# Attention and two expert layers on one core: the bias table by distance, stored with a shift per row

## The chip, the cores and the metric

One of the eight cores of a Trainium2 chip runs the whole program. The metric is the device time of one execution in microseconds (us). The kernel before was run three times: 969.26, 970.4 and 975.79 us, median 970.4. One more execution was profiled.

## The reference, cut to what matters

Three layers follow each other: attention with a learned bias, a layer of eight experts of which each token uses one, and a gated layer. The change is in the first, and there in the bias:

```python
B, H, S, D = 4, 8, 576, 64              # batch, heads, positions, head size; 32 hidden units
scores = scale * q @ k.T
psi_rel = log1p(abs(pos[:, None] - pos[None, :]))
psi_i = log1p(maximum(pos[:, None], 1.0))
x = (psi_rel / psi_i)[..., None]        # 576 x 576 x 1
h = maximum(x @ w1 + b1, 0.0)           # 576 x 576 x 32
bias = h @ w2                           # 576 x 576 x 8, the same for every batch
scores = scores + bias                  # then softmax over the last axis, and times v
```

For one query row i the bias is a function of the distance |i - j| alone; the row enters only through the factor 1 / psi_i. All data is float32.

## The kernel before, in words

**The bias stage** makes the bias of all eight heads once and puts it into three scratch tensors in device memory (`scr[0]`, `scr[1]`, `scr[4]`), from which attention loads it pair by pair of heads. There are 36 blocks of 16 query rows (`BLKS`): for c = 0 to 3 and k = 0 to 7 the rows c + 64k, c + 64k + 4, ... (every fourth row, so that c fits the order in which attention takes its rows), and for c = 4 and k = 0 to 3 sixteen adjacent rows from 512 + 16k.

For each block, `z_gen` makes four tiles z of 128 partitions (4 rows x 32 hidden units) by 576 columns: relu of a row's factor times a table of log distances, plus b1. The table stands in `ctab_sb` once per stride of rows, `toep4` and `toep1`, in a form in which a shifted window of 576 columns gives the distances of the rows at hand; the row's factor is a per-partition column of `sall`. Of the four tiles VectorE makes three (L853) and ScalarE one (L851); `ZACT` holds how many ScalarE makes, by block. On VectorE the bias is left out of the relu and made good by `off8`, a column chosen by the same number.

Three blocks later (`LA = 3`), `z_mm` multiplies the four tiles with the block-diagonal weights `w2bd` (128 x 32), each into its own 32 output partitions: 512 columns in one bank of PSUM (L866), 64 in the next (L868). That gives 16 rows x 8 heads = 128 partitions by 576. ScalarE evicts it (L875; for the last two blocks L878, with the end on VectorE, L881) into an output tile `ob`, and SyncE stores it (L872) as 128 rows of 2304 bytes. Tiles z rotate through the pools `pt0`, `E` and, in the first part of the stage (`cnt < 24`), `bias`; output tiles through `ph`, which has four buffers and is also where attention's `E` tiles come from.

`z_iter` runs `z_gen`, `z_mm` and, where `LBS` lists the iteration, one of the first pair's bias loads. 38 iterations (`Z0`) run ahead of attention, and the last one after unit 0's first scores. Between the iterations the list `extra` issues one piece each: the loads of v for the first pair (`load_v`, iterations 0 to 3), the constants of the gates (`consts`, iteration 6: two loads of the gates' weights in short pieces, one table and a memset on GpSimd), and unit 1's k and q (`load_u(0, 1)`, iterations 11 and 12). SyncE's queue issues all of these, in program order.

**Attention** takes 16 units (4 pairs of heads x 4 batches) of 5 steps. A step does the scores (L274, `s_pe`), the bias add with the row maximum on VectorE (L278, `s_max`, reading tiles of `load_bias`), the exponential on ScalarE (L283), and the transposes and the product with v of two steps earlier. Splitting q and k into a high and a low part for the next unit is GpSimd's work (L228 to L237, `prep_qk`); unit 0 runs on whole float32. Loads for later units and pairs stand in `dmaq` with due times, nine per unit, and two at most are issued in a step. `WARM` adds a few idle matmuls on the table in unit 0 (L951). After attention come the expert layer and the gated layer, whose matmuls (L598, L611, L1300, L1309, L1562) take most of the time. The order of all instructions is written out by hand.

## Time and profile before

| what | value |
|---|---|
| runs | 969.26, 970.4, 975.79 us; median 970.4 |
| profiled execution | 969.1 us, of it 967.3 us span from the first to the last instruction |
| mean granted TensorE clock | 0.999 |
| busy, share of the span | TensorE 98%, weight loads 84%, VectorE 71%, ScalarE 56%, GpSimd 12% |
| bias stage | 4.7 to 57.7 us |
| first bias add and first exponential of attention | 59.56 and 60.38 us |

Shares of the whole span mix stages with different limits; the stage of the change is 53 us of 967. In the rows below PE is TensorE's matmuls, PEld its weight loads, DVE VectorE, ACT ScalarE, POOL GpSimd, and SPq SyncE's queue, which issues the DMAs. L853 is line 853 of the kernel. A row of the timeline has the start, the time to the end of the last of its instructions, and in brackets how long the engine had been idle and on what; adjacent instructions overlap a little, so the pace is read from the starts.

### The profile page before, as it was taken

To read this page: it belongs to the slowest core of one execution; us is meant where nothing else is said; L and a number is where in the kernel's file an instruction comes from. 1 tells how busy PE (TensorE), PEld (TensorE's weight loads), DVE (VectorE), ACT (ScalarE), POOL (GpSimd) and SP (SyncE) were. 2 spreads that over 40 slices of the span, in tenths; PEclk is the share of its full clock that TensorE was granted. 3 is DMA by queue.
4 is the path that set the end of the run, shared out by engine and by line. 5 is a ranking of instruction groups with operands and counts; after the bars stand their busy time and mean duration, and the time that the engine had idled before them with its cause. 6 is when DMAs were issued, how large, how long until landed. Compare 5 with 4: busy or idle time off the path is not lost. (4 is left out here: it accounts for less than half of the span.)

```text
span 967.3 us, 19675 instructions
## 1 busy us (share of the span) xinstructions
PE 947.8 (98%) x7621; PEld 814.6 (84%) x7621; DVE 687.6 (71%) x1536; ACT 537.0 (56%) x1139; POOL 113.6 (12%) x112
## 2 busy tenths in 40 slices
PE   7999999999999999999999999999999999999997
PEld 3457777777668999999999899999999999999996
DVE  8977878878786577777556578777546677456663
ACT  8978778777775353534435443555434455345542
POOL 0954343434300000000000000000000000000000
PEclk9999999999999999999999999999999999999999
DMA  8873433343044476858654585420312510312212
GB/s 238 253 256 115 139 118 103 94 130 102 2 139 151 140 258 206 285 204 280 231 171 162 198 254 171 115 82 1 107 46 66 135 41 1 131 33 66 66 34 65
DMA packets 90815, 130.26 MB, mean 135 GB/s; under 512 B 13760, under 2 KB 48576, under 8 KB 90720
## 3 DMA queue, kind: packets, MB, share of 16 engines
q1 hardware_dynamic: 90240, 128.33, 41.4%
q8 instruction: 60, 0.98, 0.4%
q10 hardware_dynamic: 480, 0.66, 0.2%
q14 instruction: 35, 0.29, 0.1%
HBM read 93.50 MB, written 35.46 MB: 133 GB/s over the span
## 5 line engine op out<-in xcount | busy, mean ns | idle before, releaser
L278 DVE CUSTOM_DVE_ANT_0 E<-S,bias 128x576 f32<-128x576 f32 x128 | 91.8, 754 | 29.7 <-PE S L274 21.4
L283 ACT ACTIVATE E<-E,st 128x576 f32<-128x576 f32 x144 | 110.3, 769 | 1.1 <-DVE st L278 0.8
L1300 PE MATMUL Y<-fv,ws 128*128 128x384 f32 x540 | 108.8, 336 | 0.1
L1300 PEld LDWEIGHTS Y<-fv,ws 128*128 128x128 f32 x540 | 95.7, 188 | 3.2 <-issue 0.4
L385 PE MATMUL pv<-pt,rawv 128*64 128x320 f32 (+1 forms) x576 | 88.1, 422 | 0.0
L1562 PE MATMUL o<-ws,u 128*128 128x512 f32 x306 | 84.1, 394 | 0.0
L274 PEld LDWEIGHTS S<-kh,qz 64*128 64x128 f32 x540 | 52.4, 185 | 34.6 <-DVE st L278 18.9
L274 PE MATMUL S<-kh,qz 64*128 64x288 f32 x540 | 76.3, 322 | 1.6 <-DVE st L278 1.4
L600 ACT ACTIVATE qz<-T 128x288 fp32r<-128x288 f32 x63 | 25.8, 410 | 87.3 <-PE T L598 87.2
L1040 DVE TENSOR_TENSOR ws<-r,ws 128x512 fp32r<-128x512 f32 (+1 forms) x66 | 51.3, 778 | 32.0 <-ACT ws L1037 31.2
L1300 PE MATMUL X<-fr,ws 128*128 128x384 f32 x360 | 73.3, 338 | 0.0
L324 ACT ACTIVATE pt<-T 128x512 f32<-128x512 f32 (+3 forms) x112 | 50.7, 467 | 39.9 <-PE T L301 39.5
L1300 PEld LDWEIGHTS X<-fr,ws 128*128 128x128 f32 x360 | 65.0, 188 | 5.6
L1562 PEld LDWEIGHTS o<-ws,u 128*128 128x128 f32 x306 | 56.2, 188 | 6.6 <-DVE u L1355 0.4
L326 DVE COPY pt<-T 128x512 f32<-128x512 f32 (+3 forms) x112 | 55.8, 522 | 3.3 <-PE T L301 3.2
L598 PE MATMUL T<-xh,whl 128*128 128x288 f32 x256 | 56.9, 298 | 0.0
L611 PE MATMUL y<-qz,w2hl 128*128 128x288 f32 x384 | 56.5, 296 | 0.0
L611 PE MATMUL y<-qz,whl 128*128 128x288 f32 x384 | 56.4, 296 | 0.0
L601 DVE SCALAR_TENSOR_TENSOR qz<-T,qz 128x288 fp32r<-128x288 f32 x63 | 28.6, 454 | 38.4 <-ACT qz L600 37.9
L598 PE MATMUL T<-xh,w1hl 128*128 128x288 f32 x248 | 55.7, 300 | 0.0
L301 PE MATMUL T<-ident,E 64*128 64x64 f32 x1248 | 54.1, 222 | 0.0
L301 PEld LDWEIGHTS T<-ident,E 64*128 64x128 f32 x1248 | 51.2, 138 | 2.5 <-issue 0.8
(322 smaller groups left out, 2115.4 us busy)
## 6 DMA issues: line engine op xcount, KB each, us to landing
r<-wn SPq DMA_DIRECT2D x22, 512.0 KB, 4.8
bscr<-ob SPq DMA_DIRECT2D x36, 288.0 KB, 3.3
raww<-in_moe_w_dram SPq DMA_DIRECT2D x16, 512.0 KB, 6.0
bias<-bscr SPq DMA_DIRECT2D x14, 576.0 KB, 4.3
raww<-in_moe_w_dram SPq DMA_DIRECT2D x24, 256.0 KB, 4.5
raww<-in_moe_w_dram SPq DMA_DIRECT2D x8, 768.0 KB, 8.5
ro<-wn SPq DMA_DIRECT2D x22, 256.0 KB, 2.7
rawq<-in_qt_dram SPq DMA_DIRECT2D x16, 320.0 KB, 3.1
```

Source lines behind the costliest of these rows:

```text
L274: nc.tensor.matmul(t[:, f, 0:288], x[k, a], y[k, o], start=i == 0, stop=i == len(prods) - 1)
L278: nc.vector.tensor_tensor_reduce(out=E.rearrange("p (a b) -> p a b", a=2), in0=ps[:, :, 0:288], in1=bt[p, hh, c].rearrange("p (a b) -> p a ...
L283: nc.scalar.activation(E, E, AF.Exp, bias=st[:, 2 * c + hh:2 * c + hh + 1], scale=-1.0, accum_out=st[:, 10 + 2 * c + hh:11 + 2 * c + hh])
L301: nc.tensor.transpose(t[r][:, at:at + 64], E[k, o:o + 128], ident[k, k])
L324: nc.scalar.activation(o, x, AF.Copy)
L326: nc.vector.tensor_copy(o, x)
L385: nc.tensor.matmul(st["ps"][64 * hh:64 * hh + 64, 0:w], vt[p][:, hh, b, c, :], y, start=c == order[0], stop=c == order[4])
L598: nc.tensor.matmul(ps, wa[:, x, k], xs[k][y][:, o], start=k == 0 and i == 0, stop=k == 3 and i == 2)
L611: nc.tensor.matmul(hbuf["y"][d // 2][:, d % 2, 0:288], wb[:, x, d], t[:, y:y + 288], start=f == 0 and i == 0, stop=(one or f == 7) and i == 2)
L1040: return lambda: eng.tensor_tensor(l, t, h.bitcast(F32), ALU.subtract)
L1300: nc.tensor.matmul(bank, a[:, c], x[:, k], start=first and k == 0 and n == 0, stop=k == 1 and n == 2, skip_group_check=True)
L1562: nc.tensor.matmul(t, u, w, start=first and i == 0, stop=last and i == 2)
```

## The change

The table is now one row of log1p of the distances 0 to 577, after the 144 row factors, in one load. Each tile z has w columns, one for each distance that any of the block's 16 rows can have: L to the left and R to the right (`z_span`), w the larger of L + 1 and R, made even. The matmuls put the columns in order of position, L + R of them: those to the left read z backwards, those to the right forwards, with a cut at 512 for the bank of PSUM, so two or three pieces of four matmuls each. All 16 rows of a block have the same columns, and the store puts each row at its own shift: rows of the scratch tensors are 704 wide (`WB`), a row of a block 639 or 640 columns (591 for c = 4), and the row's step in memory is 704 plus the stride of the rows. Loads of the bias take columns 64 to 639 of each row; the tail's load becomes two, one per head of the pair.

Beside that, `ZACT` gives ScalarE no tile in every seventh block (VectorE makes all four there); the pool `bias` serves tiles z in blocks below 16 instead of 24; `LBS` has the first pair's four early bias loads at iterations 22, 24, 31 and 32 instead of 25, 27, 29 and 30; unit 1's k and q are issued at iteration 33; and the constants of the gates become an entry of `dmaq` with due time 27 (the first step of unit 3).

```diff
@@ -46,15 +46,14 @@
 QR, QX, QY, LP = 46, 52, 55, 6
 QL, QC = ((58, 55, 61), 58)
 F0, F1 = ((1, 2, 3, 5, 7), (0, 1, 2))
-ZACT = (1,)
-LBS = ((25, 1), (27, 0), (29, 2), (30, 3), (37, 5), (37, 6), (38, 4))
+ZACT = (1, 1, 1, 1, 1, 1, 0)
+LBS = ((22, 1), (24, 0), (31, 2), (32, 3), (37, 5), (37, 6), (38, 4))
 WARM = {1: 512, 2: 128, 3: 128}
 Z0 = 38
 
 
 BLKS = [(c, k) for c in range(5) for k in range(4 if c == 4 else 8)]
-C4, C1 = 499, 572
-W4, W1 = C4 + S, 60 + S
+TD, WB = S + 2, 704
 
 
 def both(f, g):
@@ -67,10 +66,17 @@
     return (512 + 16 * k + 4 * gq, 1) if c == 4 else (c + 4 * (16 * k + 4 * gq), 4)
 
 
+def z_span(bi):
+
+    c, k = BLKS[bi]
+    if c == 4:
+        return 527 + 16 * k, 64 - 16 * k
+    return 64 * k + (64 if k == 7 else 63), 576 - 64 * k
+
+
 def make_consts():
     r = np.repeat(np.arange(4), HID)[:, None]
-    t4 = np.log1p(np.abs(4 * r + C4 - np.arange(W4)[None, :]).astype(np.float32))
-    t1 = np.log1p(np.abs(r + C1 - np.arange(W1)[None, :]).astype(np.float32))
+    td = np.broadcast_to(np.log1p(np.arange(TD).astype(np.float32)), (128, TD))
     st = np.array([z_rows(bi, gq) for bi in range(len(BLKS)) for gq in range(4)])
     i = st[None, :, 0] + st[None, :, 1] * r
     linv = np.float32(1.0) / np.log1p(np.maximum(i, 1).astype(np.float32))
@@ -85,7 +91,7 @@
     cst2 = np.ones((128, 384), np.float32)
     cst2[:, 0:128] = np.triu(cst2[:, 0:128], 1)
     cst2[:, 128:256] = np.arange(128)
-    return {"ctab": np.concatenate([t4, linv, t1], 1).astype(np.float32), "cst": cst, "cst2": cst2}
+    return {"ctab": np.concatenate([linv, td], 1).astype(np.float32), "cst": cst, "cst2": cst2}
 
 
 def lay(inputs):
@@ -130,15 +136,13 @@
 
         ident = const.tile([128, 128], F32, name="ident")
         make_identity(nc, ident)
-        ctab_sb = ap.tile([128, NG + W4 + W1], F32, tag="pt1", bufs=2, name="ctab_sb")
-        toep4, toep1 = ctab_sb[:, 0:W4], ctab_sb[:, NG + W4:]
+        ctab_sb = ap.tile([128, NG + TD], F32, tag="pt1", bufs=2, name="ctab_sb")
+        dist = ctab_sb[:, NG:]
         w_s = const.tile([32, 10], F32, name="w_s")
         reps = ap.tile([32, 256], F32, tag="ph", bufs=EB, name="reps")
         rep_sb, w2rep = reps[:, 0:128], reps[:, 128:256]
         nc.sync.dma_start(w_s, ws)
-        for o in (slice(C4 - 48, NG + W4), slice(0, C4 - 48)):
-            nc.sync.dma_start(ctab_sb[:, o], ctab[:, o])
-        nc.sync.dma_start(toep1, ctab[:, NG + W4:])
+        nc.sync.dma_start(ctab_sb, ctab)
         cst_sb = const.tile([128, 84], F32, name="cst_sb")
         wg = const.tile([128, 4, 32], F32, name="wg")
         small = ap.tile([128, S], F32, tag="rb", bufs=1, name="small")
@@ -161,7 +165,7 @@
         for i, n in enumerate((128, 96, 64)):
             nc.scalar.activation(off8[0:n, i:i + 1], wps[0:n, 1, 0:1], AF.Copy, scale=8.0)
 
-        nc.vector.tensor_scalar(sall, ctab_sb[:, W4:W4 + NG], wcol[:, 0:1], None, ALU.mult)
+        nc.vector.tensor_scalar(sall, ctab_sb[:, 0:NG], wcol[:, 0:1], None, ALU.mult)
 
         xT = {}
         bt = {}
@@ -174,7 +178,8 @@
             def tail():
                 t = ap.tile([128, S], F32, tag="bias5", bufs=1, name="biast")
                 bt[p, 0, 4] = bt[p, 1, 4] = t
-                dq.dma_start(t, scr[4][2 * p:2 * p + 2].rearrange("h r j -> (h r) j"))
+                for h in range(2):
+                    dq.dma_start(t[64 * h:64 * h + 64], scr[4][2 * p + h, 0:64 * WB].rearrange("(r j) -> r j", j=WB)[:, 64:64 + S])
 
             def part(hh, g):
                 def f():
@@ -185,7 +190,7 @@
                         if i == 4:
                             bt[0] = pers.tile([128, NTOK], F32, tag="xT3", name="bias").rearrange("p (i a j) -> p i a j", i=2, a=2)
                         t = bt[0][:, i - 4]
-                    dq.dma_start(t, scr[g][:, 2 * p + hh].rearrange("c a j -> a c j"))
+                    dq.dma_start(t, scr[g][:, 2 * p + hh, 0:128 * WB].rearrange("c (a j) -> a c j", j=WB)[:, :, 64:64 + S])
                     for r in range(2):
                         bt[p, hh, 2 * g + r] = t[:, r]
                 return f
@@ -196,7 +201,7 @@
                         t = ap.tile([128, 2, S], F32, tag="bias", bufs=4, name="bias")
                         for i in range(2):
                             bt[p, hh, 2 + i] = t[:, i]
-                    dq.dma_start(bt[p, hh, 2 + r], scr[1][r, 2 * p + hh])
+                    dq.dma_start(bt[p, hh, 2 + r], scr[1][r, 2 * p + hh, 0:128 * WB].rearrange("(a j) -> a j", j=WB)[:, 64:64 + S])
                 return f
             rows = [part(0, 1), part(1, 1)] if p else [row(hh, r) for r in range(2) for hh in range(2)]
             return [part(0, 0), part(1, 0)] + rows[0:2] + [tail] + rows[2:]
@@ -817,7 +822,7 @@
         ld0 = load_v(0, nc.sync)
         for f in load_u(0, 0):
             f()
-        extra = ld0 + [lambda: None] * 6 + load_u(0, 1)
+        extra = ld0
 
         def consts():
             nc.sync.dma_start(cst_sb, cst)
@@ -825,28 +830,28 @@
             nc.gpsimd.memset(wg[:, :, 16:32], 0.0)
             nc.sync.dma_start(wg[:, :, 8:16], moe_w_output_gate.rearrange("(p d) e -> d p e", p=4))
 
-        extra.insert(len(extra) - 6, consts)
-
-        scr = {g: dram.tile([2, H, 128, S], F32, name=f"bscr{g}") for g in range(2)}
-        scr[4] = dram.tile([H, 64, S], F32, name="bscr4")
+
+        scr = {g: dram.tile([2, H, 129 * WB], F32, name=f"bscr{g}") for g in range(2)}
+        scr[4] = dram.tile([H, 65 * WB], F32, name="bscr4")
         zss = {}
 
         def z_gen(cnt):
             act = ZACT[cnt % len(ZACT)]
-            if cnt < 24 and cnt % 4 == 3:
+            if cnt < 16 and cnt % 4 == 3:
                 zt = [ap.tile([128, 2, S], F32, tag="bias", bufs=4, name="zk") for _ in range(2)]
                 zs = [zt[i // 2][:, i % 2] for i in range(4)]
-            elif cnt % 4 == 1 if cnt < 24 else cnt % 3 == 0:
+            elif cnt % 4 == 1 if cnt < 16 else cnt % 3 == 0:
                 zs = [ap.tile([128, S], F32, tag="E", bufs=4, name="ze") for _ in range(4)]
             else:
                 zt = ap.tile([128, 4, S], F32, tag="pt0", bufs=2, name="zp")
                 zs = [zt[:, i] for i in range(4)]
             zss[cnt] = zs
+            L, R = z_span(cnt)
+            w = max(L + 1, R)
+            w += w % 2
             for gq in (0, 3, 2, 1):
-                i0, sd = z_rows(cnt, gq)
                 g = 4 * cnt + gq
-                src = toep4[:, C4 - i0:C4 - i0 + S] if sd == 4 else toep1[:, C1 - i0:C1 - i0 + S]
-                z = zs[gq]
+                src, z = dist[:, 0:w], zs[gq][:, 0:w]
                 if gq >= 4 - act:
                     nc.scalar.activation(z, src, AF.Relu, bias=wcol[:, 1:2], scale=sall[:, g:g + 1])
                 else:
@@ -862,23 +867,28 @@
             else:
                 pt = pS.tile([128, 1024], F32, tag="S", name="bps")
                 ps = [pt[:, 0:512], pt[:, 512:1024]]
-            for gq in range(4):
-                nc.tensor.matmul(ps[0][32 * gq:32 * gq + 32, 0:512], w2bd, zs[gq][:, 0:512], start=True, stop=True)
-            for gq in range(4):
-                nc.tensor.matmul(ps[1][32 * gq:32 * gq + 32, 0:64], w2bd, zs[gq][:, 512:576], start=True, stop=True)
-            ob = ap.tile([128, S], F32, tag="ph", bufs=EB, name="ob")
+            L, R = z_span(cnt)
+            w = L + R
+            cuts = sorted({0, min(L, w), 512, w})
+            for u, v in zip(cuts, cuts[1:]):
+                for gq in range(4):
+                    z = zs[gq]
+                    x = z[:, L - v + 1:L - u + 1][:, ::-1] if v <= L else z[:, u - L:v - L]
+                    nc.tensor.matmul(ps[u // 512][32 * gq:32 * gq + 32, u % 512:u % 512 + v - u], w2bd, x, start=True, stop=True)
+            ob = ap.tile([128, WB], F32, tag="ph", bufs=EB, name="ob")[:, 0:w]
             def put():
-                dst = scr[4] if c == 4 else scr[c // 2][c % 2]
-                nc.sync.dma_start(dst[:, 16 * k:16 * k + 16, :].rearrange("h r j -> r h j"), ob)
+                dst, i0, sd = (scr[4], 512 + 16 * k, 1) if c == 4 else (scr[c // 2][c % 2], c + 64 * k, 4)
+                o = 16 * k * WB + 64 + i0 - L
+                nc.sync.dma_start(dst[:, o:o + 16 * (WB + sd)].rearrange("h (r j) -> r h j", r=16)[:, :, 0:w], ob)
 
             if not own:
-                nc.scalar.activation(ob, pt[:, 0:S], AF.Identity, bias=off8[:, act:act + 1], scale=8.0)
+                nc.scalar.activation(ob, pt[:, 0:w], AF.Identity, bias=off8[:, act:act + 1], scale=8.0)
                 put()
                 return
             nc.scalar.activation(ob[:, 0:512], ps[0], AF.Identity, bias=off8[:, act:act + 1], scale=8.0)
 
             def rest():
-                nc.vector.tensor_scalar(ob[:, 512:S], ps[1][:, 0:64], 8.0, off8[:, act:act + 1], ALU.mult, ALU.add)
+                nc.vector.tensor_scalar(ob[:, 512:w], ps[1][:, 0:w - 512], 8.0, off8[:, act:act + 1], ALU.mult, ALU.add)
                 put()
             if cnt == nb - 1:
                 late.append(rest)
@@ -903,13 +913,14 @@
 
         for cnt in range(Z0):
             z_iter()
-            n = -(-len(extra) // (Z0 - cnt))
-            for f in extra[:n]:
-                f()
-            extra = extra[n:]
+            if extra:
+                extra.pop(0)()
+            if cnt == 33:
+                for f in load_u(0, 1):
+                    f()
         dq = nc.sync
         mq = moe_early()
-        dmaq = []
+        dmaq = [(27, consts)]
         pe, ve = {}, {}
 
         def at_step(d, n, f):
...
```

## Rows read from the trace of the kernel before

**Rows 1.** Busy time of each engine by stretch, TensorE clock, DMA share and rate

```profile
core 0: us, PE busy (x) PEld busy (x) DVE busy (x) ACT busy (x) POOL busy (x), PEclk, DMA share, GB/s
4.70:57.70 53.00, 49.10 (x562) 22.74 (x564) 52.98 (x109) 50.32 (x71) 32.59 (x1) 1.00 0.87 266
30.00:42.00 12.00, 11.35 (x132) 5.45 (x131) 12.00 (x26) 11.26 (x18) 12.00 (x1) 1.00 0.71 196
44.00:55.00 11.00, 9.77 (x125) 5.56 (x123) 11.00 (x24) 10.83 (x16) 11.00 (x1) 1.00 1.01 357
80.00:100.00 20.00, 20.00 (x271) 14.40 (x268) 15.41 (x42) 15.13 (x38) 7.60 (x10) 1.00 0.45 141
```

**Rows 2.** Timeline, VectorE: the first tiles, the last ones, and what follows

```profile
4.72 1.56 DVE L853 TENSOR_SCALAR zp<-ctab_sb,sall,small 128x576 f32<-128x576 f32 x3
...
54.72 3.04 DVE L853 TENSOR_SCALAR zp<-ctab_sb,sall,small 128x576 f32<-128x576 f32 x6
57.66 0.29 DVE L881 TENSOR_SCALAR ob<-T,small 128x64 f32<-128x64 f32 x1
```

**Rows 3.** Timeline, ScalarE, one block of the bias stage

```profile
35.29 0.87 ACT L851 ACTIVATE zp<-ctab_sb,small,sall 128x576 f32<-128x576 f32 x1
36.05 0.73 ACT L875 ACTIVATE ob<-bps,small 128x576 f32<-128x576 f32 x1
36.67 0.87 ACT L851 ACTIVATE zk<-ctab_sb,small,sall 128x576 f32<-128x576 f32 x1
```

**Rows 4.** Timeline, from the bias stage to attention's first step

```profile
57.44 1.24 PE L274 MATMUL S<-rawk,rawq 64*128 64x288 f32 x8
...
59.56 0.76 DVE L278 CUSTOM_DVE_ANT_0 E<-S,bias 128x576 f32<-128x576 f32 x1 [1.61 <-DMA bscr<-ob]
...
59.79 0.69 ACT L878 ACTIVATE ob<-bps,small 128x512 f32<-128x512 f32 x1 [1.60 <-PE bps L866]
...
60.38 0.77 ACT L283 ACTIVATE E<-E,st 128x576 f32<-128x576 f32 x1
```

**Rows 5.** VectorE by line and shape: busy us and mean ns, then idle time before

```profile
L853 DVE TENSOR_SCALAR zp<-ctab_sb,sall,small 128x576 f32<-128x576 f32 x60 | 30.8, 578 | 0.0
...
L666 DVE TENSOR_SCALAR sel<-meta 128x128 f32<-128x128 f32 x5 | 1.4, 345 | 0.0
```

**Rows 6.** ScalarE by line and shape, columns as in rows 5

```profile
L324 ACT ACTIVATE pt<-T 128x512 f32<-128x512 f32 x64 | 38.3, 599 | 31.9 <-PE T L301 31.6
...
L875 ACT ACTIVATE ob<-bps,small 128x576 f32<-128x576 f32 x34 | 24.8, 731 | 1.5 <-PE bps L868 0.9 <-DMA bscr<-ob 0.5
...
L324 ACT ACTIVATE pt<-T 128x256 f32<-128x256 f32 x16 | 6.1, 382 | 7.9 <-PE T L301 7.9
```

**Rows 7.** Timeline, TensorE, one block of the bias stage

```profile
16.62 1.07 PE L866 MATMUL bps<-zk,small 128*32 128x512 f32 x8 [0.21 <-ACT ob L875]
...
17.50 0.30 PE L868 MATMUL bps<-zk,small 128*32 128x64 f32 x8
```

**Rows 8.** DMA issues: count, KB each, median us from issue to landing

```profile
bscr<-ob SPq DMA_DIRECT2D x36, 288.0 KB, 3.3
```

**Rows 9.** Timeline, GpSimd: first and last operation of unit 1's split

```profile
25.11 33.18 POOL L228 CAST kh<-rawk 128x576 fp32r<-128x576 f32 x1 [22.99 <-DMA rawk<-in_kt_dram]
...
60.52 1.55 POOL L237 TENSOR_TENSOR qz<-rawq,qz 128x640 fp32r<-128x640 f32 x1
```

**Rows 10.** Timeline: the tail's load, its first user, unit 1's first scores

```profile
64.51 0.32 SPq L177 DMA_DIRECT2D biast<-bscr  x1
...
69.95 0.76 DVE L278 CUSTOM_DVE_ANT_0 E<-S,biast 128x576 f32<-128x576 f32 x1 [0.79 <-PE Tx L301]
...
70.86 0.60 PE L274 MATMUL S<-kh,qz 64*128 64x288 f32 x4 [0.49 <-DVE st L278]
```

**Rows 11.** Timeline, SyncE's queue: the last and longest issue of the gate constants

```profile
15.51 0.63 SPq L826 DMA_DIRECT2D wg<-n_moe_w_output_gate_dram  x1
```

More of the change, by code (lines that the diff above doesn't have):

```diff
@@ L950, in body @@
                 t = pv_tile(0, "warm")
-                nc.tensor.matmul(t[:, 0:WARM[n]], ident, toep4[:, 0:WARM[n]], start=True, stop=True)
+                nc.tensor.matmul(t[:, 0:WARM[n]], ident, dist[:, 0:WARM[n]], start=True, stop=True)
             if n in pre:
```

## The prediction

> **What bounds the kernel now.** I read the busy times by stretch first [rows 1]. From 80 us on TensorE has no gap (20.00 of 20 us in the row shown, and so in the next ones), so nothing later gets shorter by itself; but the work there is issued in a fixed order, so it moves as a block when the stage ahead of it ends earlier. That stage, 4.7 to 57.7 us, makes the bias table. There VectorE is busy 52.98 of 53.00 us, ScalarE 50.32, TensorE 49.10, and the DMA engines 0.87 of their time: four resources, each near full. So I next asked which one sets the pace. VectorE issues three tiles every 1.47 us without a pause, from 4.72 until its stage ends at 57.66 [rows 2]: 52.94 us for 36 x 3 tiles, 0.490 us each. ScalarE does one tile and one eviction in 1.38 us, 0.76 and 0.62 [rows 3], and waits now and then. VectorE binds, ScalarE is 6% behind, and TensorE follows both.
>
> Then the handover to attention [rows 4]. Unit 0's first scores start at 57.44, right behind block 34's matmuls; TensorE turns to block 35, ScalarE evicts it at 59.79, and only then comes the first exponential at 60.38. VectorE's first bias add at 59.56 had waited 1.61 us for a store to free its buffer, but ScalarE's 60.38 does not hang on that. All these times hang on VectorE's end at 57.66, so what the stage gains is passed on whole.
>
> **The change, part by part.**
> VectorE's tiles. A block now needs relu only over distances 0 to w: for c below 4 the eight widths are 576, 512, 448, 384, 320, 384, 448, 514 (sum 3586), for c = 4 they are 528, 544, 560, 576 (2208). All 36 blocks together: 4 x 3586 + 2208 = 16,552 columns. Three tiles of each are VectorE's, and in every seventh block (6, 13, 20, 27, 34) also the fourth, 448 + 384 + 320 + 384 + 560 = 2096. That is 113 tiles and 51,752 columns, against 108 tiles and 62,208. The price per column is from the two rows with the same form of operation at two widths [rows 5]: (578 - 345) / 448 = 0.520 ns. So 113 x 0.490 - (113 x 576 - 51,752) x 0.00052 = 55.37 - 6.93 = 48.4 us, a gain of 4.5 us. The widths shrink by 22%, but the fixed 0.19 us of each tile and the five additional tiles stay.
>
> ScalarE. It loses five tiles (5 x 0.76 = 3.8 us), and 31 x 576 - (16,552 - 2096) = 3400 columns of the rest, at (599 - 382) / 256 = 0.848 ns, 2.9 us. Its evictions grow: 28 blocks have 639 columns, 4 have 640, 4 have 591, together 22,816 against 20,736; 2080 more at the same price is 1.8 us [rows 6]. From 36 x 1.38 = 49.7 to 44.8 us: still below VectorE. Block by block it isn't: at w = 320 VectorE needs 1.07 us and ScalarE 1.22. With no lookahead at all the larger of the two in each block would add to 50.0 us; but VectorE runs up to three blocks ahead of the matmuls, and the backlog of ScalarE never exceeds 0.4 us before a seventh block clears it. I take +0.3 us, bounds 0 and 1.6.
>
> TensorE. A block has up to three pieces instead of two, 12 matmuls instead of 8, and 634 columns on average instead of 576. The 512-column piece takes 0.88 us (16.62 to 17.50), the 64-column one 0.30 [rows 7], of which 64 x 0.88 / 512 = 0.11 is columns and 0.19 the end of the pipe. If pieces follow one another, a block takes 634 x 0.00172 + 0.19 = 1.28 us, below VectorE's mean of 1.345; if each middle piece drains, 1.47, 53 us in all, and the gain is gone. The 64-column piece starts 0.88 us after the first with 1.07 us shown for that one, so pieces do follow: 0 taken, bounds 0 and +4.6. No row shows a matmul whose moving operand is read backwards, as half of these columns are (11,392 of 22,816) and nothing in the trace says what it costs; that is a rival below.
>
> Stores. One row of a store grows from 2304 to 2556 bytes and no longer starts at a multiple of its own length. Stores land in 3.3 us [rows 8], and ScalarE waits for them 0.5 us in all [rows 6]. In the stretch of stores mostly (30 to 42 us) the DMA engines are 0.71 busy at 196 GB/s; where the bias loads join (44 to 55) they are full at 357 GB/s [rows 1]. At that rate a store of 22,816 x 512 / 36 = 324,500 bytes takes 0.91 us of all engines. With 4.56 MB of loads (the table 0.37, unit 0 0.62, v 1.18, unit 1 0.62, four bias loads 1.77), 12.8 us, the stage asks for 36 x 0.91 + 12.8 = 45.6 us of the 52 between the first load and VectorE's end: hidden, with 6 us to spare instead of the present 12 (36 x 0.83 + 14.4 of 56.5). The spreading of two bias loads helps here.
> The trace has no row of such a store, so its price is bounded in the first rival. The Trainium skill ("DMA: Bandwidth & Descriptors", How a descriptor splits into AXI transactions) says that a descriptor is cut at 256-byte boundaries and that an unaligned start costs beats for bytes that are not used; I estimate from it 88 beats for a 2556-byte row against 72 for the old one, 1.22 times instead of 1.11, about 49 us of DMA time and still hidden. No run here shows it yet.
>
> The rest. The first load is one of 361 KB where the first piece was 384 KB: 0 to -0.1 us. Unit 1's split is GpSimd work: its first cast took 33.18 us, from 25.11 until VectorE had left the stage, and the four end at 62.07 [rows 9], 8.8 us before unit 1's first scores at 70.86 [rows 10]. VectorE's last two blocks took 2.94 us with the cast waiting (54.72 to 57.66), twice the mean of all 36, so the cast cost it nothing, and loading its operands later gains nothing; behind it on GpSimd is nothing before unit 1, and only a load more than 8 us late would cost. The tail load in two halves is issued after block 35's store has landed (64.51) and is needed at 69.95 [rows 10]: 0.3 us more on SP's queue, covered by about 2 us; the other pairs have whole units of cover. The gate constants are three issues of at most 0.63 us each [rows 11]; in unit 3 they stand ahead of unit 5's loads on SP, and its memset on GpSimd, and delay them by less than 2 us and one step, with a unit (13.4 us for unit 0, 57.44 to 70.86) to cover it; in the old place they took DMA time that was not short. 0 for all of these, bounds -0.3 and +0.5.
>
> Sum: -4.5 + 0.3 - 0.1 = -4.3 us. Against the profiled execution (969.1 us, of it 967.3 span) that is 964.8. The three runs shown are 969.26, 970.4 and 975.79; the profiled one is at their lower end, the median 1.3 higher. I forecast **965.5**, own range 963 to 968.
>
> **Rivals.**
> *The DMA engines become the bound* (slower). Place: the stores of the stage, held back through the four output buffers that ScalarE waits for. It decides from (53.2 - 1.2 - 12.8) / 36 = 1.09 us of all engines for one store, 1.2 times what I reckon; at 1.22 us the whole gain is gone, and each further 0.1 us costs 3.6. At one and a half times my price (1.36 us) the stage ends near 63.0 and the kernel at 974.5, at twice near 79 and 991. For it: 0.87 share now, row starts that no store had, and less time for more bytes. Against it: 357 GB/s held for 11 us without a stall of ScalarE. 0.11 from these rows, and more than +1% in 0.06. By the Trainium skill's rule named above the spare 6 us would shrink to 3, and I would give this case 0.13.
> *Hidden gain*: TensorE's pieces drain, or ScalarE's evictions come last in most blocks, and the stage stays near 53 us: 968 to 970. For it: three engines within 10% of each other. Against: lookahead of three blocks. 0.12.
> *Backward reads at half speed*: TensorE gets 11,392 x 0.00172 = 19.6 us more, 66 us in all, and the kernel goes to about 982. Only the lack of any such row speaks for it. 0.04.
> *It does not do what it says*: narrower tiles that leave the 0.520 ns rate for twice that would put VectorE at 48.4 + 51,752 x 0.00052 = 75 us, 991; stores of skewed rows that are taken for overlapping, each waiting 3.3 us for the one before, would make the stage 36 x 3.8 = 137 us, near 1050. Widths are even and ranges of one head do not overlap, which speaks against both. 0.04.
>
> **How the numbers follow.** The forecast has 0.69. This kernel can't tell less than about 1% (9.7 us) from no change: my forecast's 4 us lie within. Faster by more than that would need twice the gain of the bound engine: 0.02. Slower by more: 0.06 + 0.03 + 0.03 = 0.12. Same: 0.86. The range begins at 962.5: if the fixed part of a narrow tile is smaller than the rows make it, VectorE falls towards ScalarE's 44.8 us, 3.6 us further, and 962.5 takes in two thirds of that. It ends at 971.5, which holds all of the hidden gain, against the median of 970.4 too, and the small end of the DMA case; 0.13 to 0.15 lie outside.
>
> **What would show it.** Right: VectorE's stage ends near 53.2 us without idle time between tiles, its row at w = 320 near 445 ns and at 576 unchanged; ScalarE's wait for stores stays below 1 us; unit 0's first exponential is near 56. Wrong: VectorE idle in the stage, waiting for TensorE (pieces or backward reads) or for a buffer; a DMA share near 1 throughout with store landings well above 3.3 us; SP's store issues one landing apart; or any later stretch where TensorE, full before, shows gaps.

## The result: 0.6% slower, where a small gain was forecast

The changed kernel takes 977.45 us (median of 8 runs, 975.53 to 979.0), the kernel before 970.63 beside it (8 runs): ratio 1.0061, 95% interval 1.0044 to 1.0078. The forecast was 965.5, with a range from 962.5 to 971.5. The profiled execution of the changed kernel took 979.0 us (span 977.2), against 969.1 (967.3); that is 9.9 us between the spans, where the medians differ by 6.8.

First the stretches, columns as in [rows 1]:

```profile
4.70:57.70 53.00, 45.53 (x792) 22.68 (x796) 48.92 (x113) 44.99 (x64) 0.00 (x0) 1.00 0.85 246
30.00:42.00 12.00, 10.60 (x196) 5.13 (x200) 11.37 (x27) 11.09 (x16) 0.00 (x0) 1.00 0.87 252
44.00:55.00 11.00, 8.09 (x148) 3.79 (x144) 8.77 (x21) 9.53 (x14) 0.00 (x0) 1.00 0.84 257
66.00:72.00 6.00, 6.00 (x17) 2.67 (x16) 1.53 (x4) 2.33 (x6) 0.00 (x1) 0.50 0.43 118
80.00:100.00 20.00, 19.83 (x262) 14.43 (x260) 15.93 (x46) 15.61 (x40) 8.51 (x12) 1.00 0.52 148
```

VectorE's work in the stage has shrunk to 48.92 us, and yet the stage is no shorter: every engine now has gaps. From 66 to 72 us TensorE ran on half its clock, where the kernel before had 1.00. VectorE by shape says that the tiles cost what was reckoned, 443 ns at 320 columns where about 445 was said and 576 at 576 [rows 5]:

```profile
L858 DVE TENSOR_SCALAR zp<-ctab_sb,sall,small 128x576 f32<-128x576 f32 x12 | 6.2, 576 | 0.0
...
L858 DVE TENSOR_SCALAR zp<-ctab_sb,sall,small 128x320 f32<-128x320 f32 x13 | 5.0, 443 | 0.1
```

VectorE's timeline shows what ate the gain, the bracket being the idle time just before and what ended it:

```profile
4.60 1.56 DVE L858 TENSOR_SCALAR zp<-ctab_sb,sall,small 128x576 f32<-128x576 f32 x3
...
28.48 1.46 DVE L858 TENSOR_SCALAR zp<-ctab_sb,sall,small 128x512 f32<-128x512 f32 x3 [1.16 <-ACT ob L885]
...
50.32 2.86 DVE L858 TENSOR_SCALAR zp<-ctab_sb,sall,small 128x514 f32<-128x514 f32 x6 [1.27 <-ACT ob L885]
...
54.67 3.49 DVE L858 TENSOR_SCALAR zp<-ctab_sb,sall,small 128x560 f32<-128x560 f32 x7
60.62 0.30 DVE L891 TENSOR_SCALAR ob<-T,small 128x79 f32<-128x79 f32 x1 [2.46 <-DMA bscr<-ob]
64.25 0.76 DVE L283 CUSTOM_DVE_ANT_0 E<-S,bias 128x576 f32<-128x576 f32 x1 [3.32 <-DMA bscr<-ob]
```

Its stage ends at 58.16 us (54.67 + 3.49), not 53.2; the longer pauses inside it hang on ScalarE's evictions. Then it waits twice for stores, and the first bias add, at 59.56 before [rows 4], comes at 64.25. ScalarE's waits name the cause (us in total, times, longest); before it was 0.5 us in all [rows 6]:

```profile
ACT ob L888 <- DMA bscr<-ob: 3.5, 2, 2.1
...
ACT ob L885 <- DMA bscr<-ob: 3.0, 4, 1.2
```

And the issues of stores; the last number is the median time to landing in us, 3.3 before [rows 8]:

```profile
bscr<-ob SPq DMA_DIRECT2D x28, 319.5 KB, 4.2
```

SyncE's queue at the handover, where unit 1's two loads now stand right ahead of the last five stores:

```profile
56.29 0.59 SPq L222 DMA_DIRECT2D rawk<-in_kt_dram  x1
56.94 0.88 SPq L222 DMA_DIRECT2D rawq<-in_qt_dram  x1
57.91 3.75 SPq L882 DMA_DIRECT2D bscr<-ob  x4
63.20 0.81 SPq L204 DMA_DIRECT2D bias<-bscr  x2
65.97 0.53 SPq L882 DMA_DIRECT2D bscr<-ob  x1
69.67 1.13 SPq L182 DMA_DIRECT2D biast<-bscr  x2
```

Last TensorE: a block of 591 columns, the wait at the handover, and unit 1's first scores (70.86 before [rows 10]):

```profile
55.84 1.19 PE L877 MATMUL bps<-ze,small 128*32 128x512 f32 x24
56.85 1.04 PE L877 MATMUL bps<-zp,small 128*32 128x512 f32 x8
...
65.07 2.96 PE L279 MATMUL S<-rawk,rawq 64*128 64x288 f32 x8 [3.60 <-DVE st L283]
...
78.60 0.60 PE L279 MATMUL S<-kh,qz 64*128 64x288 f32 x4 [0.49 <-DVE st L283]
```

The eight score matmuls that took 1.24 us at 57.44 [rows 4] take 2.96 behind a pause of 3.60 us. Unit 1 was forecast 4.3 us earlier, at 66.6; it comes 12.0 later than that: 5.0 from VectorE's stage (58.16 for 53.2), 4.0 from the handover to the first bias add (6.1 us for 2.1), 3.0 within unit 0 (14.35 us for 11.3). Of the 9.9 us between the two spans 7.7 are there by unit 1's first scores; 1.5 of the rest are lost to the clock once more, in a later step that the last section shows.

### The profile page after: what moved, and what is told of

It reads as the page before. It is cut to its first block, busy times and chain, and to the rows that moved or that the text cites. A ratio compares the mean times of both kernels' runs of the same rounds, so it can differ in the third digit from the quotient of the medians.

```text
span 977.2 us, 20181 instructions
## 1 busy us (share of the span) xinstructions
PE 950.0 (97%) x7877; PEld 817.9 (84%) x7877; DVE 684.2 (70%) x1541; ACT 532.6 (55%) x1134; POOL 81.1 (8%) x112
## 5 line engine op out<-in xcount | busy, mean ns | idle before, releaser
L616 PEld LDWEIGHTS y<-qz,w2hl 128*128 128x128 f32 x384 | 52.7, 188 | 0.5 <-ACT qz L605 0.5
```

The costliest lines, as they stand in the source:

```text
L616: nc.tensor.matmul(hbuf["y"][d // 2][:, d % 2, 0:288], wb[:, x, d], t[:, y:y + 288], start=f == 0 and i == 0, stop=(one or f == 7) and i == 2)
```

## The experiments

Three causes were on the table after the traces, and they are numbered so in the expectations of the first four runs: the shifted row starts of the stores (1), four output buffers too few for the landing of the stores (2), and the new order of loads (3). Each run stands beside runs of the kernel before, whose medians lie between 970.6 and 971.1 us from group to group. Ratios are therefore what to compare across groups; where a difference of medians is given below, the ratios say nearly the same unless the text says otherwise.

**Stores without the shift.** Same bytes, every row at a multiple of 2816 bytes.

```diff
-o = 16 * k * WB + 64 + i0 - L
-nc.sync.dma_start(dst[:, o:o + 16 * (WB + sd)]...[:, :, 0:w], ob)
+o = 16 * k * WB
+nc.sync.dma_start(dst[:, o:o + 16 * WB]...[:, :, 0:w], ob)
```

> Stores every row at a multiple of 2816 bytes, without its shift (so the bias values stand in the wrong columns), same bytes, same pieces, same order. Theory 1 (the skewed row starts make the stores slow): median landing of the stores back from 4.2 to about 3.4 us, ScalarE's waits for stores under 1 us, VectorE's stage ends near 53.5 us, ratio to the kernel before about 0.996. Theory 2 (not the addresses, but more bytes at a faster pace through a ring of four output buffers): landing stays near 4.2 us and the ratio at 1.004 to 1.008.

977.22 us, ratio 1.0067 (1.0049 to 1.0085), landing 4.0 us: as the changed kernel. The starts are not the cause. The rule of the Trainium skill that the prediction weighed ("DMA: Bandwidth & Descriptors", How a descriptor splits into AXI transactions) gives, by an estimate, 80 beats for such a row against 80 to 88 for a shifted one, by where it starts; the runs show no difference.

**Eight output buffers.** Every second block evicts into a spare tile that is idle in this stage.

```diff
-ob = ap.tile([128, WB], F32, tag="ph", bufs=EB, name="ob")[:, 0:w]
+ob = (obx[:, cnt // 2 % 4] if cnt % 2 else ap.tile([128, WB], F32, tag="ph", bufs=EB, name="ob"))[:, 0:w]
```

> The changed kernel with eight output buffers instead of four (every second one in a buffer that is idle in the bias stage). Theory 2 (four buffers of 0.8 us of eviction plus 4.2 to 5 us of landing allow a block only every 1.3 to 1.45 us): no waits for stores in ScalarE, VectorE ends near 53.5 us, the first bias add no longer waits for a landing, first exponential near 56 us, ratio about 0.996. Theory 1 (the DMA engines cannot take skewed rows as fast): the backlog only moves, the loads of the bias and the last stores land later, ratio above 1.002.

969.59, ratio 0.9985 (0.9972 to 0.9998). Stores land no sooner (4.1 and 4.6 us), but ScalarE waits for none. VectorE's timeline:

```profile
55.04 0.76 DVE L284 CUSTOM_DVE_ANT_0 E<-S,bias 128x576 f32<-128x576 f32 x1 [0.78 <-PE S L280]
...
68.69 0.76 DVE L284 CUSTOM_DVE_ANT_0 E<-S,biast 128x576 f32<-128x576 f32 x1 [3.03 <-DMA biast<-bscr]
```

The first bias add comes 9.2 us earlier than in the changed kernel, where the forecast had it, and 4.5 us earlier than in the kernel before. Unit 0 then gives most of that lead back, waiting for the tail's load: unit 1's first bias add comes at 71.11, against 72.03 in the kernel before and 79.78 in the changed one. Behind this wait TensorE's clock stood at 0.50 for 3.4 us, from 70.1 us on. Cause 2 holds, and a new wait stands behind it.

**The order of loads alone** (with the buffers of z that go with it), on the arithmetic and stores of the kernel before.

```diff
-LBS = ((25, 1), (27, 0), (29, 2), (30, 3), ...
+LBS = ((22, 1), (24, 0), (31, 2), (32, 3), ...
-extra = ld0 + [lambda: None] * 6 + load_u(0, 1)
+extra = ld0          # load_u(0, 1) at cnt == 33; constants at dmaq 27
```

> The kernel before with the new order of loads alone (unit 1's k and q at iteration 33, bias loads at 22, 24, 31, 32, gate constants in unit 3, the buffers of z), old arithmetic and old stores. Theory 3 (the late loads collide with the last stores and cost most of the loss): ratio 1.003 to 1.006, first exponential later than 60.4 us by 2 us or more. Theories 1 and 2: ratio 1.000 +- 0.002.

976.11, ratio 1.005 (1.0031 to 1.0069): the order costs 5 us without any change to the stores. The first bias add comes at 63.56, behind a wait for a store, and the clock is at 0.50 from 66 to 70 us:

```profile
63.56 0.76 DVE L278 CUSTOM_DVE_ANT_0 E<-S,bias 128x576 f32<-128x576 f32 x1 [2.92 <-DMA bscr<-ob]
```

**The change with the old order of loads** (the same lines, the other way).

> The changed kernel with the loads in the order of before. Theory 3: ratio 0.996 to 0.999, the handover waits gone. Theories 1 and 2: ScalarE still waits for stores all through the stage, ratio 1.003 to 1.006.

972.45, ratio 1.0018 (1.0006 to 1.0031). The clock is at 1.00 through the handover (it fell to 0.50 for 3.4 us inside the stage, from 51.6 us on, behind a pause of TensorE of 2.35 us), but ScalarE still waits 4.0 us for stores, and GpSimd does what it could not before. VectorE, and GpSimd's cast that took 33.18 us before [rows 9]:

```profile
26.01 3.51 DVE L860 TENSOR_SCALAR zp<-ctab_sb,sall,small 128x576 f32<-128x576 f32 x3
29.44 2.69 DVE L860 TENSOR_SCALAR ze<-ctab_sb,sall,small 128x512 f32<-128x512 f32 x3
```

```profile
26.07 0.67 POOL L233 CAST kh<-rawk 128x576 fp32r<-128x576 f32 x1 [23.95 <-DMA rawk<-in_kt_dram]
```

GpSimd's four operations ran at once, and VectorE's six tiles took 6.2 us instead of 3.0. The Trainium skill ("SBUF — State Buffer", Who interferes with whom) calls the port that the two share an exclusive lock; both traces agree, with the loser changed: GpSimd before (33.18 us), VectorE here.

**Only unit 1's loads early again**, at blocks 11 and 12.

```diff
-if cnt == 33:
-    for f in load_u(0, 1): f()
+if cnt == 11: lu = load_u(0, 1)
+if cnt in (11, 12): lu[cnt - 11]()
```

> The changed kernel with one part undone: unit 1's k and q are loaded in the middle of the stage again (blocks 11 and 12) instead of just ahead of the last four stores. Theory A (what is loaded next to the last stores delays the handover, and TensorE's pause there halves its clock): the first bias add comes from 64.3 us to about 61 to 62, TensorE pauses less than 2 us, the clock stays at 1.00 behind it, and the kernel comes down by 3 to 5 us from 977 to 972 to 974; but GpSimd then has its split's first casts from about 25 us on, and wherever VectorE waits for a store they get in, worth up to 3 us of VectorE (as in the run with the old order of loads). Theory B (the bias loads that were moved forward to blocks 22 and 24 are what delays it): no change, 976 to 978. Theory C (only the size of the stores matters): no change.

973.41, ratio 1.0029 (1.001 to 1.0048): 4.0 us back by the medians, 3.1 by the ratios, from the place of these two loads. TensorE's pause is 1.06 us, the clock behind it 1.00, GpSimd's first cast at 25.81: theory A, but for one point, that VectorE's tiles stood back to back when the cast got in. The first bias add:

```profile
61.99 0.76 DVE L283 CUSTOM_DVE_ANT_0 E<-S,bias 128x576 f32<-128x576 f32 x1 [1.49 <-DMA bscr<-ob]
```

The run before this one put back the rest of the order as well (bias loads, buffers of z, gate constants) and took 972.45, ratio 1.0018: the intervals overlap widely, so that rest is worth nothing that can be told here.

**Something for TensorE to do** in the pause.

```diff
-WARM = {1: 512, 2: 128, 3: 128}
+WARM = {0: 512, 1: 512, 2: 128, 3: 128}     # at n = 0 five times
```

> The changed kernel with five 512-column matmuls more on TensorE in the handover, whose results nobody reads; nothing else is changed. Theory A (the clock falls because TensorE has nothing to do for 3.6 us, and the slow clock costs time by itself): the granted clock stays near 1.00 from 64 to 80 us where it was 0.79 on the mean, the first bias add stays near 64.3, unit 1's first bias add comes 2 to 3.5 us earlier than 79.8, and the kernel ends at 973.5 to 975.5. Rival (the wait for the loads and stores alone makes the loss, and the slow clock lies under other waits): the clock is up and the time stays at 976.5 to 978.

975.11, ratio 1.0043 (1.003 to 1.0056). The stretch that stood at 0.50:

```profile
66.00:72.00 6.00, 6.00 (x44) 3.56 (x42) 3.56 (x9) 2.89 (x8) 0.00 (x0) 1.00 0.55 154
```

First bias add 63.85, near the 64.25 without, unit 1's first bias add 76.96 instead of 79.78. By these two times the slow clock was 2.4 us of the loss; the medians lie 2.3 us apart, the ratios 1.7, with intervals that overlap.

**Fewer bytes a row**: 576 of the columns, unshifted, 2304 bytes; first in the new order, then in the old.

```diff
-...[:, :, 0:w], ob)
+...[:, :, 0:S], ob[:, 0:S])
```

> The changed kernel, in its new order of loads, but of each evicted tile only the first 576 columns are stored, at the same places as in the run without the shift (2816 bytes apart, none shifted): 2304 bytes a row as before, where that run stored 2556. The bias values are therefore not the reference's. Theory A with the extra bytes as a part of the loss: stores land in 3.5 to 3.8 us instead of 4.1 to 4.2, ScalarE's waits for them fall by half, and the kernel is 2 to 4 us below the 977.2 of the run without the shift. Rival (order of loads alone, any bytes): 976 to 977.5, landing unchanged.

976.12, ratio 1.0055 (1.0042 to 1.0068), 1.1 us below the run without the shift, which the intervals don't tell apart. At this order's handover the bytes are not what decides.

> The change with the order of loads of the kernel before, four buffers, and only 576 of the evicted columns stored, unshifted (the bias values are not the reference's); it differs from the run with the old order of loads (972.45) by 252 bytes a row. Open is what the additional bytes cost in themselves. Theory A (landing time over four buffers, and the bytes are a part of the landing): stores land in 3.3 to 3.6 us instead of 4.2, ScalarE waits for them 0.5 to 2 us instead of 4.0, VectorE's stage ends 1.5 to 3 us earlier, 969.5 to 971. Rival (bytes are nothing, the faster pace of the stores is all): landing stays above 3.9, 972 to 973.

969.44, ratio 0.9989 (0.9977 to 1.0001), 3.0 us below the change in the old order, and landing down from 4.2:

```profile
bscr<-ob SPq DMA_DIRECT2D x35, 288.0 KB, 3.5
```

So the 252 bytes a row do cost, in the landing. ScalarE's wait in all hardly fell, though (3.8 us against 4.0). GpSimd's first cast took 6.19 us here, but that is not where the gain lies: at 41 us VectorE stands level in the two traces (41.31 and 41.19). The difference comes at its block behind 50 us, where it waits 1.36 us for an eviction instead of 2.73, and its stage ends at 58.27 instead of 60.02. The clock at 0.50 there, in the run with more bytes, may be part of that, so theory A's way is only half shown.

**Eight buffers, early loads, GpSimd held back** by a tiny copy of VectorE's last tile ahead of its split.

```diff
+if n == 0:
+    nc.gpsimd.tensor_copy(gate, zlast[0][:, 0:1])
```

> The changed kernel with eight output buffers in turn, unit 1's k and q loaded at blocks 11 and 12 again, and GpSimd's split of them held back by a small copy of VectorE's last tile, so that it cannot start inside the stage. Theory A (ring too short for landings of 4 to 5 us, plus late loads at the handover, plus GpSimd where it gets in): VectorE's stage ends at 53 to 54 without pauses, the first bias add is near 55, the tail of the bias loads does not hold up unit 0 as with eight buffers alone, unit 1's first bias add comes at 66.5 to 69, and the kernel takes 963.5 to 967. Rival (the stage's gain is taken by the bias loads behind the stores, whatever the order of unit 1's): unit 1's first bias add near 71 and 968.5 to 970 as with eight buffers alone.

969.34, ratio 0.9977 (0.9964 to 0.9991): the stage was as theory A had it, the median the rival's (the profiled execution took 967.68). SyncE's queue, then VectorE, say why:

```profile
57.48 1.66 SPq L205 DMA_DIRECT2D bias<-bscr  x2
59.26 0.53 SPq L887 DMA_DIRECT2D bscr<-obx  x1
63.60 1.13 SPq L183 DMA_DIRECT2D biast<-bscr  x2
```

```profile
56.89 0.30 DVE L896 TENSOR_SCALAR obx<-T,small 128x79 f32<-128x79 f32 x1
...
67.21 0.76 DVE L284 CUSTOM_DVE_ANT_0 E<-S,biast 128x576 f32<-128x576 f32 x1 [2.12 <-ACT pt L330]
```

The last block was ready at 57.19, its store went out at 59.26 behind two bias rows that wait for an older store, and the tail's load, which needs that store landed, at 63.60. The releaser named at 67.21 is an eviction; I took it to be the load, 3.6 us after its issue, and the next run tests that.

**The last store ahead of the bias rows.**

```diff
-... (37, 5), (37, 6), (38, 4))
+... (38, 5), (38, 6), (38, 4))
```

> As the last run (eight output buffers, unit 1's k and q early, GpSimd held back), and SP issues the last store ahead of the two bias rows that wait for an earlier block's landing, not behind them. Theory A (what is left of the loss at the handover is the last store's place on SP: issued at 59.26 us though its tile was ready near 57.2, so the tail of the bias loads went out at 63.60 and VectorE waited until 67.21): the store goes out near 57.4, the tail load near 61.5, unit 0's fifth bias add comes near 65.2, unit 1's first bias add near 67.3 instead of 69.30, TensorE's pause of 1.89 us goes, and the kernel takes 964 to 967. Rival (the rows are then late themselves, or TensorE's order sets the pace): unit 1's first bias add stays at 69 to 70, 968 to 970.

**966.49**, ratio 0.9948 (0.9931 to 0.9965), below both kernels. VectorE:

```profile
50.82 3.48 DVE L863 TENSOR_SCALAR zp<-ctab_sb,sall,small 128x560 f32<-128x560 f32 x7
...
55.30 0.76 DVE L284 CUSTOM_DVE_ANT_0 E<-S,bias 128x576 f32<-128x576 f32 x1 [0.78 <-PE S L280]
...
65.77 0.76 DVE L284 CUSTOM_DVE_ANT_0 E<-S,biast 128x576 f32<-128x576 f32 x1 [0.71 <-PE Tx L307]
...
67.86 0.76 DVE L284 CUSTOM_DVE_ANT_0 E<-S,bias 128x576 f32<-128x576 f32 x1 [0.72 <-PE S L280]
```

The tail no longer waits for its load. SyncE's queue:

```profile
57.39 0.52 SPq L887 DMA_DIRECT2D bscr<-obx  x1
...
61.75 1.13 SPq L183 DMA_DIRECT2D biast<-bscr  x2
```

Of the 2.9 us between the medians the two traces show 1.4 (unit 1's first bias add at 67.86 instead of 69.30). The rest goes along with TensorE's clock: of the twelve executions of the run before, the seven with a mean granted clock of 0.996 or 0.997 took 969.34 to 970.34, the five with 0.998 and more 965.79 to 967.91; here all six had 0.998 or more, and took 964.18 to 967.04. Where the clock fell in those seven is not shown, as only one of the five was profiled.

The stretch as in [rows 1]:

```profile
4.70:57.70 53.00, 48.43 (x848) 24.95 (x848) 50.98 (x119) 47.05 (x68) 3.08 (x5) 1.00 0.90 283
```

More bytes per us than either kernel moved there, and neither ScalarE nor VectorE waits for a store.

**The same without holding GpSimd back** (the copy left out).

> As the run beside it, but GpSimd is not held back: its split of unit 1's operands may start at 24 us as in the kernel before. Theory A (GpSimd only gets in where VectorE pauses, and with eight buffers VectorE does not): its first cast is held up as in the kernel before, VectorE's stage ends at 53.5 to 54.5, time equal to the run beside it within 1 us. Rival (it gets in at any start, so the late split was needed in itself): four casts between 24 and 32 us, VectorE's stage ends near 57, 2 to 3 us slower than the run beside it.

967.55, ratio 0.9961 (0.9948 to 0.9974). The rival's casts came, in 25.76 to 31.98 us, and VectorE's stage ended 2.3 us later:

```profile
56.55 0.29 DVE L892 TENSOR_SCALAR ob<-T,small 128x79 f32<-128x79 f32 x1
```

So GpSimd gets in even with eight buffers, and although VectorE's tiles stood back to back before it did. Unit 1's first bias add is 2.3 us later too (70.19 for 67.86). That the time differs by only 1.1 us, within the intervals, is not explained.

**The hold with four buffers** (the first bias adds wait for stores either way).

> The changed kernel with its four output buffers, unit 1's k and q at blocks 11 and 12, and GpSimd held back until VectorE's last tile. Against the same without the hold (973.4): Theory A (GpSimd's four operations cost VectorE about 3 us where it paused): 970.5 to 972. Against eight buffers with the hold (969.3): the four buffers cost 1.5 to 3 us by ScalarE's waits for stores. Rival (VectorE's lost time is covered by the waits for stores that follow): 973 to 974.

972.95, ratio 1.0029 (1.0014 to 1.0044): no different from 973.41 without it, as the rival said; VectorE's stage ends at 58.33 with the hold and 58.36 without. The profiled execution had the clock at 0.50 from 64.5 to 67.9 us, though, which that of the run without did not. Against the same with eight buffers the four cost 3.6 us by the medians, 5.0 by the ratios, and ScalarE waits 5.1 us for stores instead of none.

**The kernel before with eight buffers**, and then also with its last store ahead of the rows.

> The kernel before the change with eight output buffers and nothing else. Theory A (four buffers were enough for its pace of 1.47 us a block and landings of 3.3 us, VectorE sets the pace): 970 to 971.5, ratio 0.999 to 1.001, VectorE's stage ends at 57.4 to 57.9. Rival (the ring was short there too): the 1.6 us that the first bias add waited for a buffer is gained, 968.5 to 969.5.

968.62, ratio 0.9979 (0.9969 to 0.9988): the rival. The first bias add, without the wait of [rows 4]:

```profile
58.72 0.76 DVE L279 CUSTOM_DVE_ANT_0 E<-S,bias 128x576 f32<-128x576 f32 x1 [0.76 <-PE S L275]
```

It is 0.84 us earlier, and so is unit 1's first bias add (71.19 for 72.03); the rest of the 2.0 us does not show in the two traces.

> The kernel before the change with the same two mends as the best run so far: eight output buffers, and the last store issued ahead of the two bias rows. Open is what the change's narrower arithmetic gains by itself, once neither buffers nor the order of the last loads hold it up: the best run (966.49) has all three. Theory A (the arithmetic gains what the stage shows, 57.69 to 54.23 us for the end of VectorE's stage): this one takes 968 to 969 and the arithmetic is worth about 2 us or more. Rival (the two mends are the whole gain): 966 to 967, no difference between old and new arithmetic.

968.73, ratio 0.9976 (0.9963 to 0.9989); the place of the last store is worth nothing here (968.62 without it). With the same two mends the old arithmetic takes 968.73 and the new 966.49, ratios 0.9976 and 0.9948: narrower tiles are worth about 2 us. The new kernel also keeps the new places of the bias loads and holds GpSimd, though, and the two intervals just meet. In the traces VectorE's stage ends 3.5 us earlier (54.23 for 57.76), and unit 1's first bias add comes 3.4 us earlier (67.86 for 71.29).

**Eight buffers in the old order of loads.**

> The change's arithmetic and stores with eight output buffers and the order of loads of the kernel before. Open is whether the late order of loads costs anything once there are buffers enough. Theory A (the order costs 4 to 5 us with four buffers, and with eight about 2; against that GpSimd gets in early, worth 2): 968 to 970, no more than 1.5 us from eight buffers in the new order (969.6). Rival (the new order costs its 4 us with any buffers): 965.5 to 967.

967.51, ratio 0.9968 (0.9954 to 0.9983), against 969.59 and 0.9985 in the new order: about 2 us, between the two theories, and with intervals that overlap. With buffers enough the late loads seem to cost less than with four, but that they still cost anything is not shown. GpSimd's first cast took 18.86 us here, and the clock did not fall before the end as it did in the new order behind the wait for the tail.

## Why the prediction was wrong

**VectorE, ScalarE, TensorE: right.** Tiles cost 443 ns and 576 as said. Evictions of 639 columns took a mean of 784 ns, the 0.731 us of [rows 6] and 63 columns at 0.848 ns. TensorE did a block of 591 columns in 1.01 us (55.84 to 56.85), the 0.00172 us per column taken; this block is in three pieces, and 543 of its columns are read backwards, so neither the pieces nor the direction cost anything that shows. With nothing in its way (last-store run) VectorE's stage ended at 54.3, 1.1 us behind the 53.2 of the forecast: the coupling between the engines, taken at 0.3 us, was larger, within its bounds. The first bias add came at 55.3, as forecast.

**Stores "hidden, with 6 us to spare", and "ScalarE's wait for stores stays below 1 us": the step that failed first.** It priced a store by the rate at which all engines move bytes, and took the wrong rate: 357 GB/s, from the row with the loads. The row of stores mostly, in the same group, gives 196 / 0.71 = 276 and so 1.18 us for a store instead of 0.91, beyond the 1.09 from which its own rival was to decide. The changed kernel shows 252 / 0.87 = 290: 1.12 us, and 36 x 1.12 + 12.8 = 53.1 us asked of 52. Yet rate was not the bound: with eight buffers the stage moved 283 GB/s instead of 246 and ended at 54.3 us (last-store run). The term left out is the ring of four output buffers, used in turn: each is held for its eviction and for the landing of its store. Before, (0.73 + 3.3) / 4 = 1.01 us a block against a pace of 1.47; after, (0.78 + 4.2) / 4 = 1.25 against 1.345. The slack went from 0.46 us to 0.1, and ScalarE's waits for stores from 0.5 us to 6.5, handover included; with eight buffers they were nothing. The rival "the DMA engines become the bound" had the place right, the four buffers, and the mechanism wrong.

**"What the stage gains is passed on whole": failed.** The scores' tiles E come from the same four buffers as the evictions, so the first bias add needs a late store landed. I read its wait of 1.61 us and put it off the path; in the old kernel with eight buffers the wait was gone and unit 1 came 0.84 us earlier, so part of it was on the path. Where no store is in the way the gain is passed on: 3.5 us at the end of VectorE's stage and 3.4 at unit 1, between the two mended kernels.

**Unit 1's loads: "loading its operands later gains nothing ... only a load more than 8 us late would cost": failed on both sides.** I looked for who needs the operands, not for who stands behind them: 608 KB ahead of the last five stores, worth 3 to 4 us with four buffers. And the gain exists: in the new kernel GpSimd's split gets in between VectorE's tiles (2.3 us of the stage in the last-store run without the hold), which in the old one it never did. "The spreading of two bias loads helps" was not tried alone; with four buffers, undoing it together with the constants and the buffers of z made no difference that can be told.

**The clock was in no step.** Behind TensorE's pause of 3.60 us at the handover it stood at 0.50 for 6.8 us, about 2 us more.

**The rest.** The tail's two loads went out in 1.13 us instead of 0.32, which mattered little; what mattered was the place of the last store ahead of them, 1.4 us in the traces of the mended kernel and 2.9 in the medians, and I had not followed SyncE's order past it. Constants of the gates: nothing points to them, but no run moved them alone.

## What to carry to other kernels

Before calling a store hidden, compare (eviction + landing) / buffers with the pace per tile; here 1.25 us against 1.345 was not enough. A faster producer uses up that slack even where bytes per us would suffice. For a moved load, list what is queued behind it and what shares its buffers, not only who reads it. When a change gains nothing, look for the waits that take its place one by one: here three mends (buffers, unit 1's loads with GpSimd held, the last store) turned +0.6% into -0.5%.

## What the hardware showed unasked

- TensorE's clock fell to 0.50 (1.2 of 2.4 GHz) behind a pause of 3.60 us, and with filler matmuls it did not. A second such place lies in the routing step, where TensorE pauses 1.7 us in both kernels; the first line is the kernel before, the second the changed one:

```profile
534.38 1.64 PE L728 MATMUL qy<-whl,qz 128*128 128x512 f32 x6 [1.65 <-DVEq L1213]
535.85 2.39 PE L1309 MATMUL T<-fv,w 128*128 128x384 f32 x12
```

```profile
542.79 2.62 PE L733 MATMUL qy<-whl,qz 128*128 128x512 f32 x6 [1.72 <-issue]
545.21 2.89 PE L1320 MATMUL T<-fv,w 128*128 128x384 f32 x12
```

  The clock fell to 0.50 in one execution (543.2 to 546.6 us) and not in the other, which cost the changed kernel 1.5 us over these two rows; it fell in the mended kernel's trace too. Spans of single executions differ by that much for no reason of the change, and so do the times of one kernel: see the groups by granted clock in the last-store run.
- Shorter pauses were followed by half clock as well, in some traces: 2.35 us inside the stage (the change in the old order of loads) and 1.28 us at the handover (the hold with four buffers). A pause of 1.06 us there (unit 1's loads early) was not, nor was one of 1.89 us (eight buffers with the hold).
- Between GpSimd and VectorE the loser changes from kernel to kernel: GpSimd's first cast took 33.18, 18.86, 6.19, 2.11 or 0.67 us in five of them. GpSimd needs no pause of VectorE to get in: just before the 0.67 VectorE had stood still for 0.05 us, but where the casts of 18.86 and 2.11 got in its tiles were back to back. What decides is open.
- Skewed row starts (977.45 us against 977.22 without), and operands that TensorE reads backwards (1.01 us for 591 columns), cost nothing measurable.
- SyncE's issue of a store, 0.52 us at the median in the changed kernel, took 0.92 to 1.58 us for six of the 36.
